# Which branch body stands last, and when the last head groups' transposes are issued: an attention and gated-unit backward kernel on one core

## The chip, the cores and the metric

The kernel runs on one core of a Trainium2 chip. The metric is device time in microseconds (us), the median of several executions. The kernel before takes 4947.9 us. "The profile" is one traced execution of a kernel, some 2 us shorter than the measured time, since it counts from the first to the last instruction.

## The reference, cut to what matters

The program computes a layer and its gradients for 2048 rows of width 576: attention with 32 heads against a given K and V, times a gated unit.

```python
x = A_x
xn = _layernorm(x, axis=-1)
s = _A_ref(xn, A_k_cache, A_v_cache, A_wq, A_wo)   # softmax(q k) v, then wo; 32 heads of 128
g = _silu(_B_ref(xn, B_w_gate, B_w_up, B_w_down))
return x + s * g
...
_out, _vjp = jax.vjp(_f, A_x, A_k_cache, A_v_cache, A_wq, A_wo, B_w_gate, B_w_up, B_w_down)
return (_out0, *_grads)
```

The kernel has four stages: the gated unit forward; attention forward and backward, head by head; the gated unit backward; and last the gradients of `wq` and `wo` and of `x`, in eight groups of four heads.

Of the kernel before, what the change touches and what calls it, by code (L numbers as in the profile page):

```python
# [17 lines left out]
def ldiv(n, m):  # L18
    for d in range(min(n, m), 0, -1):
        if n % d == 0:  # L20
            return d
    return 1
# [44 lines left out]
def kernel(  # L67
# [6 lines left out]
    nc = tc.nc  # L74
# [159 lines left out]
    with tc.tile_pool(name="pa", bufs=1) as pa:  # L234
# [271 lines left out]
        with tc.tile_pool(name="a2h", bufs=3) as hp, \  # L506
# [4 lines left out]
            for sg in range(NT // SG):  # L511
# [7 lines left out]
                for sl in range(SG):  # L519
                    st = sg * SG + sl  # L520
# [343 lines left out]
                slot += 1  # L864

    flag = nc.values_load(flag_i[0:1, 0:1], min_val=0, max_val=1, skip_runtime_bounds_check_because="a comparison gives 0 or 1")
    with tc.If(flag > 0) as branch:
        attention(True)
    with branch.Else():
        attention(False)  # L870
    pdT.release()

    def late(name, bufs=1, **kw):
        return tc.tile_pool(name=name, bufs=bufs, reuse_waits="tile", **kw)
# [4 lines left out]
    HG = ldiv(H, 4)  # L879
    NHG = H // HG  # L880
    WD = ncs[-1][0] + 512
    with late("pc") as pc, late("pcf") as pcf, \
# [127 lines left out]
        def padded(pool, n, nm):  # L1010
            ts_ = [pool.tile([P, DT * P], bf, name=f"{nm}{k}") for k in range(n)]
            if KPAD:
                for t_ in ts_:
                    nc.gpsimd.memset(t_[:, D:], 0.0)
            return ts_

        def carve(t_, pat, a, b):
            v = t_.rearrange(pat)
            assert a * b <= v.shape[1]
            return v[:, :a * b].rearrange("p (a b) -> p a b", b=b)  # L1020

        HC = HG * P
        ds_all = carve(doBT[:], "p a b -> p (a b)", NT, D)
        onb0 = carve(doB[:], "p a b -> p (a b)", NT, HC)
        wqT = carve(wdT2[:], "p a b c -> p (a b c)", HG, D)

        def load_on(on_, hg):
            nc.gpsimd.dma_start(on_, rows_view(on2_d, hg * HC, HC))

        def load_dq(dq_, hg):  # L1030
            nc.gpsimd.dma_start(dq_, rows_view(dq2_d, hg * HC, HC))
# [16 lines left out]
        def turn_rows(dst, src, a, b, n):  # L1048
            nc.sync.dma_start_transpose(dst[:, a * n:b * n, :], src[:, a:b, :].rearrange("p t f -> p (t f)"))  # L1049
# [111 lines left out]
        with late("c2w") as wp, late("c2b") as blk, late("c2s", 2) as sb, late("c2ps", 4, space=PSUM) as ps:  # L1161
            dqTs = padded(wp, 2, "dqT")
            onqs = [(onb0, dqb_at.get(0)), tuple(blk.tile([P, NT, HC], bf, name=nm)[:] for nm in ("onb", "dqb"))]
            if not dqb_at:
                onqs[0] = (onb0, carve(ah0[:], "p a t f -> p (a t f)", NT, HC))
                load_dq(onqs[0][1], 0)
            NTE = NT // 2 if NHG > 1 else 0
            if NHG > 1:
                load_on(onqs[1][0], 1)
                load_dq(onqs[1][1], 1)  # L1170
            dqbT = blk.tile([P, NT * HG, P], bf, name="dqbT")
            dqbT2 = blk.tile([P, max(1, NTE) * HG, P], bf, name="dqbT2")
            wqT2 = blk.tile([P, HG, D], bf, name="wqT2")

            def dx_more(st, both=False):
                acc = ps.tile([P, WD], f32, name="acc")
                terms = [(dqbT[:, st * HG + hl, :], wqT[:, hl, :]) for hl in range(HG)]
                if both:
                    terms += [(dqbT2[:, st * HG + hl, :], wqT2[:, hl, :]) for hl in range(HG)]
                dx_row(acc, st, terms)  # L1180
                return acc

            gots = {}

            def load_got(st):
                gots[st] = sb.tile([P, D], bf, name="got")
                nc.gpsimd.dma_start(gots[st][:], go2[st * P:(st + 1) * P, :])

            def finish(st, acc):
                tot = sb.tile([P, D], f32, name="tot")  # L1190
                cs = sb.tile([P, 2], f32, name="cs")
                junk = sb.tile([P, D], f32, name="junk", bufs=1)
                nc.vector.scalar_tensor_tensor(tot[:], acc[:, :D], 1.0, dxn[:, st, :], op0=ALU.mult, op1=ALU.add, accum_out=cs[:, 0:1])  # L1193
                nc.vector.scalar_tensor_tensor(junk[:], tot[:], 1.0, xn_all[:, st, :], op0=ALU.mult, op1=ALU.mult, accum_out=cs[:, 1:2])  # L1194
                m12 = sb.tile([P, 2], f32, name="m12")
                nc.vector.tensor_scalar(m12[:], cs[:], -1.0 / D, None, op0=ALU.mult)
                nb_ = sb.tile([P, 1], f32, name="nb")
                nc.vector.tensor_tensor(nb_[:], m12[:, 0:1], rstd_all[:, st:st + 1], op=ALU.mult)
                t = sb.tile([P, D], f32, name="t")
                nc.vector.scalar_tensor_tensor(t[:], xn_all[:, st, :], m12[:, 1:2], tot[:], op0=ALU.mult, op1=ALU.add)  # L1200
                nc.scalar.activation(t[:], t[:], AF.Identity, bias=nb_[:], scale=rstd_all[:, st:st + 1])  # L1201
                dx = sb.tile([P, D], bf, name="dx")
                nc.vector.tensor_tensor(dx[:], t[:], gots.pop(st)[:], op=ALU.add)  # L1203
                nc.gpsimd.dma_start(o1[st * P:(st + 1) * P, :], dx[:])

            NQ = max(1, NT // 4)
            for hg in range(NHG):
                cols = slice(hg * HC, (hg + 1) * HC)
                onb, dqb = onqs[hg % 2]
                final = hg == NHG - 1  # L1210
                early = hg == NHG - 2
                ends = list(range(NTE)) if early else list(range(NTE, NT)) if final else []
                nc.sync.dma_start_transpose(wqT, A_wq[:, cols])  # L1213
                def turn_dq(a, b):
                    for a_ in range(a, b, NQ):
                        turn_rows(dqbT, dqb, a_, min(a_ + NQ, b), HG)
                turn_dq(NTE if final else 0, NTE if early else NT)
                if early:
                    nc.sync.dma_start_transpose(wqT2[:], A_wq[:, (hg + 1) * HC:(hg + 2) * HC])
                    turn_rows(dqbT2, onqs[(hg + 1) % 2][1], 0, NTE, HG)  # L1220
                dwq = wp.tile([P, DT, HC], bf, name="dwq")
                for st in ends[:2]:
                    load_got(st)
                nsteps, step_n = 2 * HG, 0
                wait_n = min(3 if early else 1, nsteps - 2)
                todo_rows = list(ends)
                held = []

                def ends_rows():
                    if todo_rows and step_n >= wait_n:  # L1230
                        for _ in range(-(-len(todo_rows) // max(1, nsteps - step_n - final))):
                            if todo_rows:
                                st = todo_rows.pop(0)
                                finish(st, dx_more(st, early))
                                if st + 2 <= ends[-1]:
                                    load_got(st + 2)
                for hl in range(HG):
                    h = hg * HG + hl
                    lcols = slice(hl * P, (hl + 1) * P)
                    accumulate(ps.tile([P, WD], f32, name="acc"), dqb, xn_all, lcols, dqTs[h % 2])  # L1240
                    nc.sync.dma_start_transpose(dwq[:, :, lcols], dqTs[h % 2][:])
                    if early and hl == min(1, HG - 1):
                        turn_dq(NTE, NT)
                    if final and hl == HG - 1:
                        store_T(out_4, cols, dwq)
                    step_n += 1
                    ends_rows()
                    dwo = sb.tile([P, D], bf, name="dwo")
                    accumulate(ps.tile([P, WD], f32, name="acc"), onb, ds_all, lcols, dwo)
                    nc.gpsimd.dma_start(out_5[h * P:(h + 1) * P, :], dwo[:])  # L1250
                    step_n += 1
                    if hl < HG - 1:
                        ends_rows()
                if not final:
                    if hg + 2 < NHG:
                        load_on(onb, hg + 2)
                        load_dq(dqb, hg + 2)
                    store_T(out_4, cols, dwq)
                    for st in range(len(ends), NT):
                        acc = dx_more(st)  # L1260
                        nc.vector.tensor_tensor(dxn[:, st, :], acc[:, :D], dxn[:, st, :], op=ALU.add)
                while todo_rows:
                    step_n = nsteps
                    ends_rows()
# [30 lines left out]
```

## The kernel before: what the change touches

Attention exists twice in the program. The usual body uses no maximum in the softmax, which is safe if a bound on the scores is small. A flag computed on the chip says so. On these inputs the usual body always runs.

```python
flag = nc.values_load(flag_i[0:1, 0:1], min_val=0, max_val=1, ...)
with tc.If(flag > 0) as branch:
    attention(True)       # the usual body
with branch.Else():
    attention(False)      # the general body
```

Right after it the next stage starts: rows of `o` are transposed by DMA, and the rows of `wo` of the last nine heads (in the tiles Kn, Vn, dOn) are loaded, behind a tiny pacing copy that holds the third `o` row back.

```python
for st in range(1, R0):
    if st > 1:
        nc.gpsimd.tensor_copy(oTs[st][0:1, 0, 0:1], loads[0][st % 3][0:1, 0:1])
    load_oT(oTs[st], st)
for view, h0, n, dead in wo_parts:
    if dead in (1, 2, 3):
        load_wo_rows(view, h0, 0, n)
```

The last stage, for each group `hg` of four heads. `wqT` holds transposed weights and `dqbT` transposed rows of dq; both come by transposing DMAs that SyncE issues, one after another.

```python
nc.sync.dma_start_transpose(wqT, A_wq[:, cols])
...
turn_dq(NTE if final else 0, NTE if early else NT)
if early:                     # the last but one group also does half the rows of the last
    nc.sync.dma_start_transpose(wqT2[:], A_wq[:, (hg + 1) * HC:(hg + 2) * HC])
    turn_rows(dqbT2, onqs[(hg + 1) % 2][1], 0, NTE, HG)
...                           # 8 accumulations of 3.9 us, with rows of dx between them
if hg + 2 < NHG:
    load_on(onb, hg + 2)      # 2 MB each
    load_dq(dqb, hg + 2)
```

## Time and profile before

| | before |
|---|---|
| median of 4 runs | 4947.94 us (4942.96 to 4948.41) |
| span of the profiled run | 4943.5 us |
| TensorE busy | 4877.6 us |
| fetch gap at the end of attention | 4.3 us on TensorE, 7.0 us on GpSimd |
| waits for transposed dq in the last two groups | 3.8 and 2.4 us |

The lines themselves stand in the prediction below. How to read them: TensorE (PE in the profile) is busy for 4877.6 of 4943.5 us, so a change is worth what it takes from the time in which TensorE stands still or runs at half clock (the granted clock is 0.50 from 3544 to 3546 us, after the gap at the end of attention, and 1.00 from 3530 to 3542 us). Time on any other engine counts only if TensorE waits for it. In the lines, PEld is TensorE's loading of weights, ACT is ScalarE, DVE VectorE, POOL GpSimd, and SPq the queue of SyncE.

### The profile page before, as it was taken

The numbers are of one execution on the slowest core, as the hardware profiler recorded it, in microseconds if no ns is written. First come the engines' busy times: TensorE is split into PE (matmuls) and PEld (weight loads), VectorE is DVE, ScalarE is ACT, GpSimd is POOL, SyncE is SP. The second block draws the span as 40 slices with busy tenths as digits, with TensorE's granted clock in tenths as the row PEclk, the third lists the DMA queues.
The fourth block names the chain that finished last, engine by engine and source line by source line (L and its number), as shares of the span: only waits on it lengthen the run. The fifth ranks groups of instructions, "written<-read, shape, count | busy, mean of one in ns | idle before, by whom it ended". The sixth has DMA issues, their size and how long they took to land. (4 is left out here: it accounts for less than half of the span.)

```text
span 4943.5 us, 101621 instructions
## 1 busy us (share of the span) xinstructions
PE 4877.6 (99%) x41029; PEld 2892.8 (59%) x41029; DVE 2802.9 (57%) x6554; ACT 2473.9 (50%) x4228; POOL 843.4 (17%) x1329
## 2 busy tenths in 40 slices
PE   9999999999999999999999999999899999999998
PEld 4445666666666666666666666666455555555554
DVE  4544666666566666666656666666434555554225
ACT  4431766766676676676666667667312111111011
POOL 3322111111111111111111111111221111111111
PEclk9999999999999999999999999999999999999999
DMA  7887999999999999999999999999999999998665
GB/s 260 274 202 173 225 222 225 228 229 230 222 231 224 230 225 237 219 227 220 235 220 231 233 224 229 231 221 231 210 225 235 223 234 218 233 226 204 195 168 151
DMA packets 3048181, 1097.68 MB, mean 222 GB/s; under 512 B 2951890, under 2 KB 2956115, under 8 KB 3047699
## 3 DMA queue, kind: packets, MB, share of 16 engines
q1 hardware_dynamic: 2948930, 771.66, 83.4%
q0 software_dynamic: 98160, 318.85, 20.3%
q8 instruction: 322, 5.28, 0.4%
q14 instruction: 161, 1.31, 0.1%
q10 hardware_dynamic: 608, 0.59, 0.0%
HBM read 175.31 MB, written 177.93 MB: 71 GB/s over the span
## 5 line engine op out<-in xcount | busy, mean ns | idle before, releaser
L654 ACT ACTIVATE Pq<-sp 128x1024 bf16<-128x1024 f32 x1024 | 1048.0, 1024 | 268.7 <-PE sp L636 259.4
L709 DVE SCALAR_TENSOR_TENSOR Pq<-dp,negdelta,Pq 128x1024 bf16<-128x1024 f32 x512 | 655.2, 1280 | 44.5 <-PE dp L706 44.5
L712 ACT ACTIVATE t<-dp,negdelta 128x1024 bf16<-128x1024 f32 x512 | 567.6, 1115 | 214.3 <-PE dp L706 199.8
L636 PE MATMUL sp<-KQ 128*128 128x512 bf16 x2048 | 609.6, 379 | 2.2 <-ACT Pq L654 2.1
L706 PE MATMUL dp<-VT,dOT 128*128 128x512 bf16 x2048 | 609.2, 379 | 2.3
L683 PEld LDWEIGHTS <-dST 128*128 128x128 bf16 x8192 | 506.8, 98 | 155.5 <-DMA dST<-Pq 16.3
L683 PEld LDWEIGHTS <-PT 128*128 128x128 bf16 x8192 | 499.8, 98 | 133.6 <-DMA PT<-Pq 14.1
L683 PE MATMUL acc<-Kn,dST 128*128 128x128 bf16 x8192 | 556.3, 219 | 9.0 <-DMA dST<-Pq 8.8
L683 PE MATMUL acc<-Vn,PT 128*128 128x128 bf16 x8192 | 542.0, 219 | 8.6 <-DMA PT<-Pq 8.3
L713 DVE TENSOR_TENSOR Pq<-t,Pq 128x1024 bf16<-128x1024 bf16 x512 | 354.6, 693 | 319.3 <-ACT t L712 307.0
L744 PE MATMUL acc<-Pq,dOn 128*128 128x512 bf16 x2048 | 531.1, 379 | 0.0
L744 PE MATMUL acc<-Pq,Qn 128*128 128x512 bf16 x2048 | 526.7, 380 | 0.0
L724 ACT ACTIVATE dq_n<-acc,rsc 128x128 bf16<-128x128 f32 x512 | 187.7, 367 | 335.1 <-PE acc L683 313.6
L1154 DVE TENSOR_TENSOR dxn<-acc,dxn 128x576 f32<-128x576 f32 x272 | 206.1, 758 | 248.1 <-PE acc L1054 248.1
L744 PEld LDWEIGHTS <-Qn 128*128 128x128 bf16 x2048 | 200.4, 98 | 240.8 <-issue 1.5
L744 PEld LDWEIGHTS <-dOn 128*128 128x128 bf16 x2048 | 198.9, 98 | 233.8
L1116 ACT ACTIVATE ndh<-dh 128x512 bf16<-128x512 f32 x144 | 86.0, 597 | 452.5 <-DVE du_blk L1114 448.7
L641 DVE TENSOR_REDUCE rs_all<-rsp 128x1 f32<-128x2 f32 x512 | 78.4, 153 | 306.4 <-ACT Pq L654 294.8
L636 PEld LDWEIGHTS <-KQ 128*128 128x128 bf16 x2048 | 179.3, 98 | 124.4 <-issue 4.0
L706 PEld LDWEIGHTS <-dOT 128*128 128x128 bf16 x2048 | 178.7, 98 | 124.6 <-issue 12.4
L677 POOL DMA_DIRECT2D on_d<-o_n x128 | 97.4, 761 | 784.3 <-DVE junk L695 460.3
L677 POOL DMA_DIRECT2D dq_d<-dq_n x128 | 98.2, 768 | 721.4 <-ACT dq_n L724 681.7
(208 smaller groups left out, 6827.6 us busy)
## 6 DMA issues: line engine op xcount, KB each, us to landing
out_dram<-kvn POOLq DMA_DIRECT2D x64, 512.0 KB, 4.8
ah<-a_d POOLq DMA_DIRECT2D x18, 1024.0 KB, 9.3
ah<-h_d POOLq DMA_DIRECT2D x18, 1024.0 KB, 11.7
h_d<-h_row POOLq DMA_DIRECT2D x64, 256.0 KB, 3.5
a_d<-a_row POOLq DMA_DIRECT2D x64, 256.0 KB, 3.9
x_all<-in_A_k_cache_dram SPq DMA_DIRECT2D x64, 256.0 KB, 4.0
on_d<-o_n POOLq DMA_DIRECT2D x128, 128.0 KB, 4.6
kvT_d<-KQ POOLq DMA_DIRECT2D x32, 512.0 KB, 5.7
```

Of the source, the lines that this page charges most:

```text
L636: nc.tensor.matmul(sp[:, c * CH:(c + 1) * CH], lhsT=hs.QT[:, qt * P:(qt + 1) * P], rhs=hs.KT[:, hf * HW_ + c * CH: hf * HW_ + (c + 1) * CH ...
L654: nc.scalar.activation(Pq[:, hsl], sp[:], AF.Exp, scale=SCALE, accum_out=hs.rsp[:, hf:hf + 1])
L677: nc.gpsimd.dma_start(dst_d[q0 * P:(qt + 1) * P, hs.h * P:(hs.h + 1) * P].rearrange("(t p) d -> p t d", p=P), buf[:])
L683: nc.tensor.matmul(hs.acc[:, 0, :], lhsT=T[:, kt, :], rhs=rhs[:, kt, :], start=(kt == 0), stop=(kt == NT - 1))
L706: nc.tensor.matmul(dp[:, c * CH:(c + 1) * CH], lhsT=hs.dOT[:, qt * P:(qt + 1) * P], rhs=hs.VT[:, hf * HW_ + c * CH: hf * HW_ + (c + 1) * C ...
L709: nc.vector.scalar_tensor_tensor(Pq[:, hsl], dp[:], hs.negdelta[:, qt:qt + 1], Pq[:, hsl], op0=ALU.add, op1=ALU.mult)
L712: nc.scalar.activation(t[:], dp[:], AF.Identity, bias=hs.negdelta[:, qt:qt + 1], scale=1.0)
L713: nc.vector.tensor_tensor(Pq[:, hsl], t[:], Pq[:, hsl], op=ALU.mult)
L724: nc.scalar.activation(hs.dq_n[:, qt % G4, :], hs.acc[:, 0, :], AF.Copy, scale=hs.rsc[:, qt:qt + 1])
L744: nc.tensor.matmul(self.acc, lhsT=self.nat[:, qt, :], rhs=self.slabs[qt][:, cs], start=(qt == self.lo), stop=(qt == self.hi - 1))
L1116: nc.scalar.mul(ndh[:], dh[:], -1.0)
L1154: nc.vector.tensor_tensor(dxn[:, st, :], acc[:, :D], dxn[:, st, :], op=ALU.add)
```

## The change

It has two parts with one intent: to remove the last places where TensorE waits for something that could have come sooner. The first lets the usual body stand last, so that its end runs straight into the next stage, where there was a jump over the general body. The second issues the transposes for the last group a group sooner, and uses their weights again instead of loading them a second time.

```diff
-    with tc.If(flag > 0) as branch:
+    with tc.If(flag < 1) as branch:
+        attention(False)
+    with branch.Else():
         attention(True)
-    with branch.Else():
-        attention(False)
...
+            def last_turns():
+                nc.sync.dma_start_transpose(wqT2[:], A_wq[:, (NHG - 1) * HC:])
+                turn_rows(dqbT2, onqs[(NHG - 1) % 2][1], 0, NTE, HG)
...
-                nc.sync.dma_start_transpose(wqT, A_wq[:, cols])
+                if not (final and NTE):
+                    nc.sync.dma_start_transpose(wqT, A_wq[:, cols])
...
-                if early:
-                    nc.sync.dma_start_transpose(wqT2[:], A_wq[:, (hg + 1) * HC:(hg + 2) * HC])
-                    turn_rows(dqbT2, onqs[(hg + 1) % 2][1], 0, NTE, HG)
...
-                                finish(st, dx_more(st, early))
+                                finish(st, dx_more(st, early, wqT2[:] if final and NTE else wqT))
...
+                if hg == NHG - 3:
+                    last_turns()
```

More of the change, by code (lines that the diff above doesn't have):

```diff
@@ L1173, with dx_more @@
             wqT2 = blk.tile([P, HG, D], bf, name="wqT2")
-            def dx_more(st, both=False):
+            def last_turns():
+                nc.sync.dma_start_transpose(wqT2[:], A_wq[:, (NHG - 1) * HC:])
+                turn_rows(dqbT2, onqs[(NHG - 1) % 2][1], 0, NTE, HG)
+            def dx_more(st, both=False, w=wqT):
                 acc = ps.tile([P, WD], f32, name="acc")
-                terms = [(dqbT[:, st * HG + hl, :], wqT[:, hl, :]) for hl in range(HG)]
+                terms = [(dqbT[:, st * HG + hl, :], w[:, hl, :]) for hl in range(HG)]
                 if both:
@@ L1206 @@
             NQ = max(1, NT // 4)
+            if NHG == 2:
+                last_turns()
             for hg in range(NHG):
@@ L1261 @@
                         nc.vector.tensor_tensor(dxn[:, st, :], acc[:, :D], dxn[:, st, :], op=ALU.add)
+                if hg == NHG - 3:
+                    last_turns()
                 while todo_rows:
```

## The prediction

> **What bounds the kernel now.** I read the page first. It says that TensorE decides nearly everything: 99% of the span is matmul, so only what makes TensorE stand still, or run at a lower clock, can be won. Span minus PE busy is 4943.5 - 4877.6 = 65.9 us for the whole program.
>
> ```profile
> span 4943.5 us, 101621 instructions
> PE 4877.6 (99%) x41029; PEld 2892.8 (59%) x41029; DVE 2802.9 (57%) x6554; ACT 2473.9 (50%) x4228; POOL 843.4 (17%) x1329
> ```
>
> The waits view of PE (columns: who waits, for whom, us in total, times, longest) then says where it stands still. Two of its lines belong to the two parts of the change; two more hang on the first.
>
> ```profile
> PE acc L1054 <- DMA dqbT<-dqb: 6.2, 2, 3.8
> PE acc L958 <- issue: 5.4, 2, 4.3
> PE acc L958 <- DMA Vn<-in_A_wo_dram: 3.8, 1, 3.8
> PE acc L958 <- DMA Kn<-in_A_wo_dram: 1.8, 1, 1.8
> ```
>
> Then the timeline around the end of attention (start us, us long, engine, line, operation, in brackets the idle time before it and what ended it). "issue" means that no semaphore explains the idle time. TensorE does 20 matmuls, stands for 4.31 us, then runs slowly; GpSimd stands for 6.98 us.
>
> ```profile
> 3536.07 2.61 PE L958 MATMUL acc<-dsT,KQ 128*128 128x512 bf16 x20 [1.07 <-issue]
> ...
> 3542.99 2.81 PE L958 MATMUL acc<-dsT,KQ 128*128 128x512 bf16 x14 [4.31 <-issue]
> ...
> 3543.62 0.56 POOL L933 DMA_DIRECT2D dsg<-dsg_d  x1 [6.98 <-issue]
> ...
> 3560.08 1.60 PE L958 MATMUL acc<-Vn,KQ 128*128 128x512 bf16 x6 [3.77 <-DMA Vn<-in_A_wo_dram]
> ```
>
> The packets of the instruction queues (page part 3 lists them, q8 in 16 KB packets, q14 in 8 KB ones) settle what this is: one 16 KB packet at 3539.6 us lasting 2.0 us, and three 8 KB packets at 3539.4 to 3539.6. The engines had run out of instructions. They jump from the end of the first branch body over the second, which for PE is 53,720 instructions long.
>
> The entry into attention, by contrast, falls through, and nothing of the kind is seen: PE goes straight on, and its first wait is for ScalarE.
>
> ```profile
> 483.24 0.59 PE L636 MATMUL sp<-KQ 128*128 128x512 bf16 x2
> ...
> 485.07 1.28 ACT L612 ACT_TABLE_LOAD   x1 [1.29 <-PE acc L215]
> ...
> 487.63 0.59 PE L636 MATMUL sp<-KQ 128*128 128x512 bf16 x2 [2.12 <-ACT Pq L654]
> ```
>
> Last, the timeline of the two last head groups, where SyncE issues transposing DMAs one behind the other.
>
> ```profile
> 4830.01 3.62 SPq L1213 DMA_TRANSPOSE wdT<-in_A_wq_dram  x1
> ...
> 4833.73 3.80 SPq L1049 DMA_TRANSPOSE dqbT<-ah  x2
> ...
> 4837.58 2.33 SPq L1219 DMA_TRANSPOSE wqT<-in_A_wq_dram  x1
> ...
> 4840.01 4.33 SPq L1049 DMA_TRANSPOSE dqbT<-dqb  x1
> ...
> 4846.52 1.16 PE L1054 MATMUL acc<-wqT,dqbT 128*128 128x512 bf16 x8 [3.80 <-DMA dqbT<-dqb]
> ...
> 4890.54 2.14 SPq L1213 DMA_TRANSPOSE wdT<-in_A_wq_dram  x1
> ...
> 4896.82 2.13 PE L1054 MATMUL acc<-wdT,dqbT 128*128 128x512 bf16 x16 [2.39 <-DMA dqbT<-dqb]
> ```
>
> [...] after 3.80 us of waiting the next 24 matmuls take 4.79 us in the chain of waits, where 24 take 24 x 15.68/128 = 2.94 us at full clock; after the 2.39 us wait they keep full speed. [...]
>
> **The change part by part.** No arithmetic is added or removed. The order of instructions, laid side by side, is the same on every engine inside both attention bodies; after them SyncE has one DMA fewer (367 instead of 368) and four rows in another order.
>
> *A. Exit from attention.* The usual body now stands last. A branch instruction still ends it, but its target is the next instruction. Removed from PE: 1.07 + 4.31 = 5.4 us standing, and the slow stretch after it: 26 matmuls from 3542.99 to 3547.8 took 4.85 us, at half clock, so some 2.4 us more. What counts, though, is what comes next: PE then waits for Kn, Vn and dOn rows, which GpSimd loads after a pacing copy at 3547.43. So the gain is what GpSimd gains. It finishes its last store at 3536.64 and could go on at once instead of at 3543.62: up to 6.9 us. Its row loads would now queue behind a 512 KB store in flight (it landed 7.6 us after issue) and the transposes of xnT, so I take off 1 us: the copy comes at about 3541.4, and Kn, Vn and dOn land as long after it as now (7.5 to 12 us). The waits for Kn and Vn, 5.6 us, stay. Gain 6 us, between 4 and 7.
>
> *B. Entry.* The jump moves here, and all five engines take it. Each fetch costs (from the exit: packet landed at 3541.6, PE on at 3543.0) about 1.4 us after landing, plus 0.3 to 2 us of packet[...]. Around 482 us only GpSimd's stores are moving, and no transposes, so I estimate 2.5 to 3 us for an engine, not 7. PE would start at about 485 instead of 482.9, but its next wait is for ScalarE anyway (2.12 us). ScalarE ends its last work at 483.79 and loads its table only at 485.07, since it also waits for stores issued at 482.2; so about 1.3 us of its fetch is hidden. Net delay 1.4 us through ScalarE[...]. [...] Cost 2.5 us, between 0.5 and 5.
>
> *C. Last head groups.* Today, between 4830.0 (the group before has done with its weights) and PE's need of the first row at 4842.7, SyncE must issue 3.62 + 3.80 + 2.33 + 4.33 = 14.1 us of transposes. After: the weights of the last group go out at about 4812, when SyncE is idle. The turn of its dq rows needs a load issued at 4817.0 that lands 14.3 us later by the tile view of dqb:
>
> ```profile
> L1031 POOL DMA_DIRECT2D dqb<-dq_d x1: 1163/1163/1163, 4817.0 to 4817.0; - x1
> ...
> DMA to landing us min/median/max: 14.3/14.3/14.3
> ```
>
> So it starts at 4831.3, no sooner than PE frees the weights, and holds SyncE for 4.3 us (to 4835.7). Weights of the group, 2.5 to 3.6 us, follow to 4838.2 to 4839.4; the first turn is issued then and lands 4.0 us later (as the one at 4892.77 did): 4842.2 to 4843.4, against a need at 4842.7. The wait shrinks from 3.80 to 0 to 0.7 us, and with it the 1.85 us of half clock (4.79 - 2.94). Gain 5.65 less 0.4, say 5.2, between 3 and 5.7.
>
> In the last group the reload of weights (2.14 us) is gone, because the weights lie in a second tile. The first turn need no longer wait for the last row of the previous group, so it can go out some 4 us earlier. The 2.39 us wait vanishes: gain 2.4. VectorE then still has eight rows of 4.36 us = 34.9 us, which today run from 4898.0 to 4932.9 without a break, so the end follows VectorE's first row, and that moves with PE's. The tail after it (ScalarE's last casts, the dwq transpose, stores) is unchanged. C together: 7.6 us.
>
> **Sum.** -6 + 2.5 - 7.6 = -11.1 us; 4947.64 - 11.1 = 4936.5. The rivals are mostly on the small side, so I say 4937.
>
> **The rivals.**
> 1. *The jump is only moved.* The fetch at the entry costs as much as at the exit (PE 5.4 us and 2.4 us of low clock). For it: all engines fetch at once[...]. Against it: little DMA traffic and a ScalarE wait that hides some. A and B then cancel, leaving C: 4940.
> 2. *The branch that ends the second body still refetches*, although its target is adjacent. [...] A is then nothing and B is paid: 4947.64 + 2.5 - 7.6 = 4942.5.
> 3. *Head-of-line blocking on SyncE.* The early turn waits for its 2 MB load, and the weights stand behind it in the same queue. If that load lands at 4835 rather than 4831.3, the first turn lands at about 4846.5 as today, and only the 2.4 us of the last group remain: 4942.
> 4. *A second hidden wait at the exit:* rows queue behind the 512 KB store, and A gains only 3 us: 4940.
>
> **Range and chances.** Taking the low ends (A 7, B 0.5, C 8.1) gives 4933; A 4, B 5, C 5.4 gives 4943. The three times of the kernel before differ by 5.3 us among themselves, so I widen to 4930 to 4945. All this is 0.2% of the span; neither rival comes near 2% (99 us). Faster by over 2%: 0.01; within 2%: 0.98; slower: 0.01.
>
> **What would show it.** A right: no "issue" gap on the first L958 matmuls, GpSimd's first row load about 0.1 us after its last store, waits for Kn and Vn still there. B right: instruction packets at about 482 to 486 us, an "issue" gap of 2 to 3 us on PE, table load at about 486.5. C right: the L1054 wait for dqbT under 1 us in total, matmuls after it at full speed, one weight transpose fewer. I am wrong if the gap at the entry exceeds 5 us, if the exit keeps its gap, or if the early turn holds up the weights beyond 4840.

B's 2.5 us of cost were 1.4 us through ScalarE and about 1 us for a lower TensorE clock; this second term was the author's estimate. The sum: -6 + 2.5 - 7.6 = -11.1 us.

## The result, and the profile after

The changed kernel takes 4934.34 us (4931.75 to 4937.6, 4 runs) against 4947.94 us. The ratio is 0.9975, with a 95% interval of 0.9958 to 0.9992. A ratio here is the mean time of one kernel's runs over that of the other's runs of the same rounds, so it is not quite the ratio of the medians. The gain of some 12 to 14 us is real but small.

The page of the profile after, its first lines:

```profile
span 4929.9 us, 100847 instructions
...
PE 4835.4 (98%) x40273; PEld 2894.6 (59%) x41029; DVE 2802.5 (57%) x6554; ACT 2472.1 (50%) x4228; POOL 840.7 (17%) x1329
```

Careful here: PE busy fell by 42 us, more than the span. But 756 matmul records are missing (40273 of 41029), so this row shows nothing of the change. Weight loads (PEld) are complete in both, so I compare the traces by the start of the same weight load in each.

The waits view of PE after (who waits, for whom, total us, times, longest):

```profile
PE sp L636 <- issue: 5.2, 2, 2.7
PE acc L958 <- DMA Kn<-in_A_wo_dram: 2.8, 1, 2.8
PE acc L958 <- DMA Vn<-in_A_wo_dram: 2.8, 1, 2.8
PE acc L1054 <- DMA dqbT<-ah: 1.6, 1, 1.6
...
PE acc L958 <- issue: 0.2, 1, 0.2
```

The "issue" wait has moved from L958 (the exit from attention) to L636 (the entry). The dqbT waits, 6.2 us in two before, are one of 1.6 us.

The timeline at the entry, after:

```profile
485.50 0.39 PE L636 MATMUL sp<-KQ 128*128 128x512 bf16 x1 [2.50 <-issue]
486.52 1.28 ACT L612 ACT_TABLE_LOAD   x1 [2.86 <-DMA dsg_d<-dsg]
...
488.56 0.61 PE L636 MATMUL sp<-KQ 128*128 128x512 bf16 x1 [2.67 <-issue]
...
489.20 1.02 ACT L654 ACTIVATE Pq<-sp 128x1024 bf16<-128x1024 f32 x1 [1.18 <-PE sp L636]
```

TensorE stops twice: after the branch, and again after one matmul. 16 KB instruction packets begin at 482.5 and 486.2 us, within these two gaps. ScalarE's first exponential starts at 489.2, where before it started at 486.5.

The timeline at the exit, after:

```profile
3533.59 4.33 PE L958 MATMUL acc<-dsT,KQ 128*128 128x512 bf16 x33
...
3534.85 0.55 POOL L756 DMA_DIRECT2D kvT_d<-VT  x1 [1.81 <-DVE VT L754]
...
3535.39 0.55 POOL L933 DMA_DIRECT2D dsg<-dsg_d  x1
...
3552.16 1.60 PE L958 MATMUL acc<-Vn,KQ 128*128 128x512 bf16 x6 [2.76 <-DMA Vn<-in_A_wo_dram]
```

TensorE runs on at full speed (33 matmuls in 4.33 us, granted clock 1.00 from 3533 to 3540 us), and GpSimd issues its next load the moment its last store is out. The waits for the `wo` rows in Kn and Vn are still there.

The exit before, shown in the prediction, had two fetches as well. TensorE's branch is on record there at 3532.25 us for 3.65 us, with a 16 KB packet at 3533.2; after it TensorE stood only 1.07 us. The gap of 4.31 us came 41 instructions later (20 matmuls, 21 weight loads), with the next packet at 3539.6. In turns_only and reload_only (below) it comes after the same 41 instructions. So this stop seems tied to its place in the program, as the second stop at the entry is, which padding removes (pad, below). No run here moves the one at the exit, so its cause is not shown.

The timeline of the last but one group, after:

```profile
4824.37 4.64 SPq L1049 DMA_TRANSPOSE dqbT<-dqb  x1
...
4829.11 2.29 SPq L1220 DMA_TRANSPOSE wdT<-in_A_wq_dram  x1
...
4831.45 4.96 SPq L1049 DMA_TRANSPOSE dqbT<-ah  x2
...
4836.22 1.15 PE L1054 MATMUL acc<-wdT,dqbT 128*128 128x512 bf16 x8 [1.62 <-DMA dqbT<-ah]
```

(The tile names are those of reused memory: wdT is the weight tile, ah the dq rows.) SyncE now has three jobs in this stretch instead of four, and has issued the last by 4836.4. The matmuls after the short wait run at full speed, 8 in 1.15 us.

From the aligned weight loads, in us. "Entry" is from the last weight load before the branch to the 120th after it; "attention" from there to its last weight load; "exit" from there to the first of the gated unit's backward stage; then that stage and the first six groups; the last two groups; and the end.

```
                 entry attention    exit  middle   group6  group7     end     span
before            22.3    3029.3   147.4  1148.0     60.5    41.5    11.7   4943.5
after             24.0    3026.5   141.5  1148.0     56.7    39.0    11.6   4929.9
```

So: entry +1.7, exit -5.9, the last two groups -3.8 and -2.5, together -10.5 us. The rest of the 13.6 us comes from attention itself (-2.8), in which the two kernels do the same; the repeated run below shows that this part is chance.

### The profile page after: what moved, and what is told of

The parts are those of the page before. It is cut to its first block, busy times and chain, and to the rows that moved or that the text cites. A ratio compares the mean times of both kernels' runs of the same rounds, so it can differ in the third digit from the quotient of the medians.

```text
span 4929.9 us, 100847 instructions
## 1 busy us (share of the span) xinstructions
PE 4835.4 (98%) x40273; PEld 2894.6 (59%) x41029; DVE 2802.5 (57%) x6554; ACT 2472.1 (50%) x4228; POOL 840.7 (17%) x1329
## 4 chain that ended last, share of the span: by engine, by line
PE 94%; DMA 2%; DVE 2%; issue 1%; ACT 1%; SPq 0%; POOL 0%; POOLq 0%; ACTq 0%; DVEq 0%
PE acc L683 18%; PE acc L744 18%; PE acc L998 13%; PE acc L1054 8%; PE dp L706 8%; PE sp L636 8%; PE acc L215 6%; PE u_ps L450 3%; PE dh L1111 3%; PE g_ps L448 3%; PE acc L533 3%; PE acc L958 2%; PE acct L145 1%; DMA dST<-Pq 1%; DVE Pq L709 1%
## 5 line engine op out<-in xcount | busy, mean ns | idle before, releaser
L706 PE MATMUL dp<-VT,dOT 128*128 128x512 bf16 x1919 | 581.6, 379 | 2.4
L683 PEld LDWEIGHTS <-PT 128*128 128x128 bf16 x8192 | 500.1, 98 | 130.9 <-DMA PT<-Pq 11.1
L636 PE MATMUL sp<-KQ 128*128 128x512 bf16 x1858 | 568.9, 380 | 5.2 <-issue 5.2
L636 PEld LDWEIGHTS <-KQ 128*128 128x128 bf16 x2048 | 179.3, 98 | 127.7 <-issue 7.2
```

The source lines that it names most:

```text
L636: nc.tensor.matmul(sp[:, c * CH:(c + 1) * CH], lhsT=hs.QT[:, qt * P:(qt + 1) * P], rhs=hs.KT[:, hf * HW_ + c * CH: hf * HW_ + (c + 1) * CH ...
L683: nc.tensor.matmul(hs.acc[:, 0, :], lhsT=T[:, kt, :], rhs=rhs[:, kt, :], start=(kt == 0), stop=(kt == NT - 1))
L706: nc.tensor.matmul(dp[:, c * CH:(c + 1) * CH], lhsT=hs.dOT[:, qt * P:(qt + 1) * P], rhs=hs.VT[:, hf * HW_ + c * CH: hf * HW_ + (c + 1) * C ...
```

## The experiments

Theory: the jump costs a fetch wherever it is taken, and it is cheaper at the entry than at the exit; the two parts of the change act each on its own stretch and add. Rivals: the jump is only moved and gains nothing; the branch instruction itself costs, wherever its target; SyncE's queue, not the transfers, sets the time of the turns.

The table collects every trace, in the columns explained above. The middle is left out: it is 1148.0 us everywhere but in all_three, where it is 1148.6. The last column is the last part of attention, 1200 weight loads in the last head.

```
                 entry attention    exit   group6  group7     span  last head
before            22.3    3029.3   147.4     60.5    41.5   4943.5      142.8
after             24.0    3026.5   141.5     56.7    39.0   4929.9      141.4
after_again       24.4    3031.9   140.5     56.1    39.0   4934.2      145.0
branch_only       24.2    3040.4   141.2     62.0    43.4   4952.5      147.3
turns_only        21.2    3030.5   148.0     56.8    39.0   4937.6      144.7
reload_only       21.3    3038.7   148.3     61.6    39.0   4951.2      147.2
no_else           21.3    3023.4   146.7     56.8    39.0   4929.4      142.6
pad               26.1    3023.3   141.0     58.8    39.0   4931.0      144.6
dq_first          24.5    3027.0   139.7     56.7    39.0   4929.6      142.9
defer_on          24.3    3024.6   138.9     54.9    39.0   4924.0      139.9
late_rows         24.6    3034.6   134.8     56.8    39.2   4932.1      145.1
all_three         24.1    3028.4   129.8     56.6    39.3   4921.7      144.6
rows_defer        24.3    3037.1   129.8     54.9    39.0   4927.7      150.8
pad_rows_defer    24.8    3032.9   129.8     54.9    39.0   4923.4      149.0
```

### The two parts, each alone: branch_only and turns_only

branch_only is the kernel before with this edit and nothing else:

```diff
-    with tc.If(flag > 0) as branch:
-        attention(True)
-    with branch.Else():
-        attention(False)
+    with tc.If(flag < 1) as branch:
+        attention(False)
+    with branch.Else():
+        attention(True)
```

> Only the order of the two attention bodies is swapped; the last head groups stay as in the kernel before. My theory (entry costs about 1.7 us in the aligned traces, exit gains about 7.2 us): net 5 to 6 us faster than before apart from the attention part itself, whose own waits moved by up to 4 us either way between the two first traces; no 'issue' gap of over 0.3 us on the first L958 matmuls, two 'issue' gaps on L636 of 2.5 to 2.7 us each, and the two dqbT waits of 3.8 and 2.4 us still there. Rival 'the jump is only moved': net 0 to 1 us.

turns_only is the changed kernel with that edit undone.

> Only the turns of the last head groups are changed; the usual body stays first and jumps at its end. My theory: the two dqbT waits (3.8 and 2.4 us) become one of about 1.6 us, no half clock after it, and the last two groups end 6 to 7 us sooner; the exit keeps its 'issue' gap of some 4 us on L958 and 7 us on GpSimd. Net 6 to 7 us faster than before. Rival: the gain hangs on the shifted phase of the exit, then under 4 us.

Measured: branch_only 4940.19 us, ratio to before 0.9988 (0.9972 to 1.0005); turns_only 4939.25 us, ratio 0.9987 (0.9971 to 1.0004). Each is a gain of some 6 us, and each interval just reaches 1, so the times alone don't settle it. The traces do. In branch_only the entry is 24.2 and the exit 141.2, as in the changed kernel, while the last groups are as before or worse. In turns_only it is the other way round. Its waits of PE:

```profile
PE acc L958 <- issue: 5.3, 2, 4.2
...
PE acc L1054 <- DMA dqbT<-ah: 1.7, 1, 1.7
```

The fetch gap at the exit is back, and the dqbT wait is the short one. The two ratios fall short of 1 by 0.0012 and 0.0013, together 0.0025, which is what the whole change has. With intervals of 0.0017 to either side, so exact a sum is luck; that each part changes its own stretches, and only it does, is what the traces show.

The profiled run of branch_only was its slowest (4954.25; the other three 4936.66 to 4943.13). It shows where the scatter is: its attention took 3040.4 us, 11 more than before.

### Half of the second part: reload_only

The kernel before, in which the last group uses the second weight tile and doesn't load its weights again; the early turns stay where they were.

```diff
-                nc.sync.dma_start_transpose(wqT, A_wq[:, cols])
+                if not (final and NTE):
+                    nc.sync.dma_start_transpose(wqT, A_wq[:, cols])
...
-                                finish(st, dx_more(st, early))
+                                finish(st, dx_more(st, early, wqT2[:] if final and NTE else wqT))
```

> Of the head group part only this: the last group uses the second weight tile and does not load its weights again; the early turns stay where they were. My theory: the 2.4 us wait in the last group goes to 0 (1.9 us or more gained there), the 3.8 us wait and the half clock after it stay. Rival: the wait in the last group is one for the dq turn itself, issued when the last row is done; then 2 us of it stay.

Measured: one look, 4952.96 us, with an attention of 3038.7. The last group takes 39.0 us, just as in the whole change, and the wait in it is gone; the one in the group before it stays:

```profile
PE acc L1054 <- DMA dqbT<-dqb: 4.1, 1, 4.1
```

So the last group's 2.5 us come from not loading the weights again, and the 3.8 us of the group before come from issuing the turns sooner.

### Is it the branch or the distance: no_else

The changed kernel without the general body. It is no usable kernel, but on these inputs its result is right. The compare-and-branch and the closing branch are still there.

```diff
-    with tc.If(flag < 1) as branch:
-        attention(False)
-    with branch.Else():
-        attention(True)
+    with tc.If(flag > 0):
+        attention(True)
```

> The changed kernel with the general body left out altogether: compare-and-branch and the closing branch remain, but neither goes far (the result stays right on these inputs; it is no usable kernel). If the cost at the entry is the fetch of a distant target: no 'issue' gap on L636, ScalarE's first exponential at about 486.4 us instead of 489.2, and everything up to the first head 1.7 us sooner than in the changed kernel; exit as in the changed kernel. Rival (the branch instruction itself flushes what was fetched): a gap of 2.5 us or more stays at the entry.

Measured: 4931.65 us, ratio 0.9975. At the entry:

```profile
484.77 1.28 ACT L612 ACT_TABLE_LOAD   x1 [1.27 <-DMA dsg_d<-dsg]
...
487.32 0.59 PE L636 MATMUL sp<-KQ 128*128 128x512 bf16 x2 [2.10 <-ACT Pq L654]
```

No "issue" gap is left, and the entry takes 21.3 us, as in the two kernels with the usual body first (21.2 and 21.3; 22.3 in the first trace of before). Which branches there are the traces tell too (`--source L867`; on TensorE, in before, after and no_else; ns shortest, median and longest, then first and last start):

```profile
L867 PEldq COMPARE_BRANCH  x2: 92/1870/3647, 481.5 to 3532.3; - x2
...
L867 PEldq COMPARE_BRANCH  x1: 4018/4018/4018, 481.4 to 481.4; - x1
...
L867 PEldq COMPARE_BRANCH  x2: 87/136/185, 481.2 to 3525.1; - x2
```

The two records of 3.65 and 4.02 us are the jumps over a whole body. At the entry of before and no_else the branch falls through (92 and 87 ns). The closing branch of no_else goes nowhere far (185 ns on TensorE, 38 to 51 on the others), and no fetch gap follows. The changed kernel has no branch at the exit at all. So it is the jump over the body that costs, not the branch instruction. The fetch at the entry costs 24.3 - 21.5 = 2.8 us (the mean of the seven unpadded kernels that jump there, and of the four that don't).

A miss: the exit should have been 141 us and was 146.7, with no fetch gap. The waits for Kn and Vn were 4.9 and 8.9 us there; the Vn rows landed 18.8 us after their issue, against 10.7 in the changed kernel. Why, no run here tells. This cost 5 us, more than the 2.8 us that leaving out the jump gained; that no_else still ran as fast as the changed kernel goes with its attention of 3023.4 us.

### The second stop at the entry: pad

TensorE stopped again after one matmul, with a 16 KB packet before each of its two stops (482.5 and 486.2 us). If the second stop hangs on where the target of the jump lies among these packets, moving the target would remove it. That was a guess. The edit adds 16 instructions to the general body, which never runs:

```diff
+            if not fast:
+                pad = acc_tile(bf)
+                for _ in range(8):
+                    nc.tensor.transpose(pad[:, 0, :], ident[:], ident[:])
```

> The changed kernel with 16 more TensorE instructions (8 transposes that never run) at the end of the general body. In the changed kernel PE stopped twice at the entry, after 0 and after 2 instructions, with an instruction packet before each[...]. Theory: with the target moved 16 on, [...] one 'issue' gap of about 2.5 us stays and the second one (2.7 us) goes; the first 120 weight loads after the entry take about 22.8 us instead of 24.0, since ScalarE (table load near 486.5) then binds. Rival: ScalarE's and GpSimd's fetches bind anyway, then no change in the 24.0 us.

Measured: one look, 4932.76 us. The second stop is gone, as the two PE lines with a wait at the entry show:

```profile
485.49 0.59 PE L636 MATMUL sp<-KQ 128*128 128x512 bf16 x2 [2.41 <-issue]
...
489.19 0.59 PE L636 MATMUL sp<-KQ 128*128 128x512 bf16 x2 [1.60 <-ACT Pq L654]
```

So it went, here and in the two later kernels with padding: each has one gap, where the seven unpadded kernels with a jump at the entry have two. So where the target lies matters here; why it does is not shown. The gain did not come: the entry took 26.1 us, not 22.8. ScalarE's table load began at 486.6, as without padding (486.5). Its own fetch is the likely cause: the profile puts the 2.86 us in the changed kernel down to a store, but behind the same store, without a jump, no_else loaded at 484.77. ScalarE's first exponential came 1.2 us sooner (488.0 against 489.2), but TensorE then waited 3.4 us for the first transposes of P, which it had not done in the changed kernel. In the two later kernels with padding the entry took 24.1 and 24.8. So the rival stands: removing a stop that wasn't the last to end gained nothing here.

### What bounds the early turns: dq_first and defer_on

In the changed kernel SyncE stood until 4824.4 for a 2 MB load of dq rows, while TensorE had been done with the old weights at about 4822.8. That looked like head-of-line blocking. dq_first puts that load first:

```diff
-                        load_on(onb, hg + 2)
                         load_dq(dqb, hg + 2)
+                        load_on(onb, hg + 2)
```

> The changed kernel with the two loads for the group after next in the other order, dq rows before o rows. Theory (head-of-line blocking: SyncE stood until 4824.4 for the dq load issued second, while PE had freed the weights at 4822.8): the dq load lands some 5 us sooner, the remaining 1.6 us wait for dqbT goes to 0 to 0.3 us, and the stretch of the last but one group falls from 56.7 to 55.1 us. Rival: the o rows, now second, land too late for the group's second accumulation, and a new wait of 1 to 3 us appears on L998; or the transposes themselves are too slow and 1 us or more stays.

Measured: one look, 4931.43 us. The load landed after 9.0 us instead of 14.5, and SyncE started the early turn at once:

```profile
4817.39 11.38 SPq L1049 DMA_TRANSPOSE dqbT<-dqb  x1
...
4828.87 2.17 SPq L1220 DMA_TRANSPOSE wdT<-in_A_wq_dram  x1
```

The turn now took 11.38 us instead of 4.64 and ended at the same time as before (the weights follow at 4828.9; in the changed kernel, 4829.1). The wait stayed at 1.7 us. My theory fell: the order of the two loads is not the bound. The new theory is that the 2 MB load of o rows beside the turn takes the bandwidth: the turn got 6.7 us longer when that load was issued second. defer_on tests it by moving that load of the last group behind the turns:

```diff
+                        if hg != NHG - 3:
+                            load_on(onb, hg + 2)
-                        load_on(onb, hg + 2)
...
                     if early and hl == min(1, HG - 1):
                         turn_dq(NTE, NT)
+                        load_on(onqs[(NHG - 1) % 2][0], NHG - 1)
```

> The changed kernel with the load of the last group's o rows (2 MB) put off until after the turns of the group before last. Loading dq first did not help: the load landed 5 us sooner, but the early turn then took 11.4 us instead of 4.6 and ended at the same time. Theory: what bounds the turns is the DMA engines' throughput between about 4808 and 4829 us, shared with the 4 MB of loads. Then with 2 MB taken out of that stretch the dqbT wait (1.6 us) goes to 0 to 0.3 and the stretch of the last but one group falls from 56.7 to 55.1 us, if the o rows still land before the last group needs them. Rival: SyncE's own issue time of the transposes bounds; then 1 us or more of the wait stays.

Measured: one look, 4925.77 us.

```profile
4815.23 4.23 SPq L1049 DMA_TRANSPOSE dqbT<-dqb  x1
...
4830.40 1.15 PE L1054 MATMUL acc<-wdT,dqbT 128*128 128x512 bf16 x8
```

The turn is about as short as it was in before (4.23 us, against 4.33), TensorE has no wait before its first row, and the group takes 54.9 us instead of 56.7. The o rows landed 10.2 us after their later issue, and the last group is unchanged at 39.0. So the DMA engines' throughput bounds the turns here, as expected: 11.38 us with the o load moved behind the dq load, 4.23 with it out of the stretch. In dq_first the DMA engines were full from 4812 to 4828 us (mean busy share of 1.01 to 1.25 in each 4 us, as the profile counts it). There one transfer was sooner at the other's cost: the dq load took 5.5 us less to land than in the changed kernel (9.0 against 14.5), the turn 6.7 us more (11.38 against 4.64).

### The waits behind the exit: late_rows, and the edits together: all_three

The exit still had 5.5 us of waiting for `wo` rows in Kn and Vn and 1.2 us for the third `o` row, and half clock after them (6 matmuls in 1.60 us; at full clock 0.90). late_rows loads these rows within the last head, where the other 23 heads' rows are loaded already, and drops the pacing copy.

```diff
-                if dead in (1, 2, 3):
-                    continue
                 view_h0[id(view)] = h0
...
-                if st > 1:
-                    nc.gpsimd.tensor_copy(oTs[st][0:1, 0, 0:1], loads[0][st % 3][0:1, 0:1])
                 load_oT(oTs[st], st)
-            for view, h0, n, dead in wo_parts:
-                if dead in (1, 2, 3):
-                    load_wo_rows(view, h0, 0, n)
```

> The changed kernel with the last nine heads' rows of wo loaded inside the last head's attention, as the other 23 are, and without the pacing copy before the third transposed row of o. Theory: the waits for Kn, Vn and xn_all after the exit (2.8, 2.8, 1.2 us) and the half clock that follows them go, and the stretch from the last attention matmul to the first of the next stage falls from 141.5 us to about 131; net 9 to 11 us faster than the changed kernel, some 20 us than before. Rival: the loads delay the transposes of the last head (more dST waits there), or the third o row becomes the wait instead (over 4 us on xn_all); then under 4 us.

all_three is the changed kernel with pad, dq_first and late_rows together.

> The changed kernel with the three edits together (16 instructions of padding, dq loads first, wo rows inside attention). If each acts alone on its own stretch, the gains add: about 1 + 1.6 + 10 us, so some 12 us under the changed kernel and 24 us (0.5%) under the one before. If one is absorbed by another, under 8 us.

Measured: late_rows 4937.03 us (4929.36 to 4940.49), ratio to before 0.9971; all_three 4926.7 us (4920.73 to 4927.64), ratio 0.9949 (0.9936 to 0.9963). The three waits are gone in both, and the exit falls from 141.5 to 134.8 and 129.8 us. In late_rows one new wait appears some 28 us into the exit:

```profile
3569.74 5.64 PE L951 MATMUL acc<-dsT,KQ 128*128 128x512 bf16 x31 [3.26 <-DMA KQ<-on_d]
```

The o row after those came late there; in the three other kernels with this edit it didn't. The net gain of late_rows over the changed kernel, expected at 9 to 11 us, can't be seen in its times: its attention took 3034.6 us, 8 more than in the first trace of the changed kernel. all_three shows the expected 24 us against before (0.9949 of 4951 is 25 us less), but two of its three edits did nothing by themselves, so chance in attention is part of it.

### What repeats, and a version that may beat both: after_again, rows_defer, pad_rows_defer

after_again is the changed kernel, unedited.

> The changed kernel once more, unedited, for a narrower interval and to see what repeats. Theory: about 0.25% faster than the kernel before; entry (first 120 weight loads) 24 us, exit to the next stage 141 us, last two groups 56.7 and 39.0 us, as in its first trace, while the attention in between differs by several us from the first trace. Rival: these stretches vary as much as the attention does, and the split of the gain was luck.

rows_defer is the changed kernel with late_rows and defer_on.

> The changed kernel with both edits that are left: the wo rows loaded inside attention (exit stretch 134.8 and 129.8 us instead of 141.5 in the two runs that had it) and the o rows' load put off. Theory: 8 to 13 us under the changed kernel of the same call, some 20 to 25 us (0.4 to 0.5%) under the one before. Rival: the extra loads lengthen the waits for dST in the last head and give back what the exit gained; then under 5 us.

Measured, 5 rounds: after_again 4936.02 us, ratio 0.9974 (0.9961 to 0.9988); rows_defer 4929.64 us, ratio 0.9966 (0.9952 to 0.9979). Before ran between 4940.14 and 4955.13 in the same rounds. after_again repeats the first result, and its stretches too: 24.4, 140.5, 56.1, 39.0. Its attention took 3031.9 us, 2.6 more than before, where the first trace had 2.8 less. So attention scatters by itself. The traces' attention runs from 3023.3 to 3040.4 us; the scatter of the times (15 us for before) is of that size.

rows_defer has both stretches as expected (129.8 and 54.9), but its last head took 150.8 us, and the 6 us between the two medians fall short of the expected 8 to 13. Is that chance, or do the extra loads lengthen it? pad_rows_defer, with the padding added, asks again.

> The version with wo rows inside attention and the late load of o rows, plus the 16 instructions of padding. Theory: padding gives nothing (in both runs that had it, ScalarE's fetch and table load set the entry), so this is the version without it again: ratio to the kernel before 0.995 to 0.997, exit stretch 118.1 + 11.7 us, last but one group 54.9 us, and the last head's stretch, 150.8 us without padding, back within the 140 to 147 us of the other runs if that value was chance. Rival: the loads of wo rows do lengthen the last head; then it is above 148 us again.

Measured: 4926.02 us (4925.34 to 4935.43), ratio 0.9965 (0.995 to 0.9981). Its last head took 149.0 us, so by what I had written down the rival holds. The four kernels that load the rows inside the last head took 145.1, 144.6, 150.8 and 149.0 us there, mean 147.4; the ten others 139.9 to 147.3, mean 143.8. Some 3.5 us of the 12 us that the exit gained are given back in the last head. With so few traces and such scatter this is likely, not certain.

So rows_defer, with or without padding, is faster than before. Against the changed kernel it is better by its stretches and its median, by some 6 us against after_again in the same rounds, but the two intervals overlap: that it is faster is likely, not shown.

## Why the prediction was right

**Size.** 4937 us was said, with 4930 to 4945; 4934.34 was measured. "Within 2%" was right.

**A, exit.** Said: 6 us gained, the waits for Kn and Vn unchanged at 5.6 us. The exit stretch lost 5.9 us, and the two waits sum to 5.5. The way there was right too: the pacing copy came 4.8 us after GpSimd's last store (3540.22 against 3535.40), as the prediction had it. What the copy and the row loads take after the store, and not TensorE's own gap with its half clock, set the gain. Two readings were wrong without harm. The half clock had cost some 1.7 us, not 2.4: 26 matmuls took 4.85 us, and at the full clock, in the changed kernel, 46 take 5.6, so 26 take 3.2. And no branch ends the second body; the changed kernel's trace has none there.

**B, entry.** Said: cost 2.5 us, TensorE on at 485, table load at 486.5. Measured: 485.5 and 486.52; the cost is 1.7 us against the first trace of before and 2.8 us between the means of the kernels with and without a distant jump there. GpSimd stood 4.00 us, more than the 2.5 to 3 estimated for an engine; whether less DMA traffic makes it shorter than the 6.98 us at the exit is not shown. The granted clock was lower: 0.58 on average from 486 to 494 us, against 0.79 in before. A second stop, named as a possibility in a passage now cut, did come after two instructions (2.67 us, with a 16 KB packet at 486.2 us), and pad shows that removing it gained nothing. One reading doesn't hold: in before the profile puts ScalarE's wait of 1.29 us down to TensorE, not to the stores, of which the last had landed 2.6 us after its issue, at 484.8. Rival 1 fails by its size. Rival 2 can't be judged from the changed kernel, which has no closing branch, but no_else has one, with a near target and no fetch gap. Rival 4 fails too: Kn landed 7.1 us after its issue, where it took 7.5 before.

**C, last groups.** The last group's 2.4 us came as 2.5. The last but one gained 3.8 us where 5.2 was said, still within the stated 3 to 5.7. Here two terms were mis-sized. The need was put at 4842.7, when TensorE began to wait before. But before, it had already done the first 8 matmuls of that row and waited for the second half; now what lands last is needed by the first 8, so the need is 1.0 us sooner. And the first turn landed 4.8 us after issue (4831.45 to 4836.2), not 4.0. The two make 1.8 us; the wait was 1.62. The start and duration of the early turn were as said (14.5 us to land, 4.64 us to turn). The half clock went with the wait: the granted clock was 0.74 on average from 4846.5 to 4853 us in before, after 3.80 us of waiting, and is 1.00 from 4830 to 4846.5 us in the changed kernel, around the 1.62 us. Rival 3, blocking in the queue, looked likely from this trace, but dq_first and defer_on (turns of 11.38 and 4.23 us) show that bandwidth is behind it.

**The sum.** -11.1 us was said. The four stretches give -10.5. That this is so near is partly luck: C fell 1.3 us short, and B cost 0.8 us less in this trace. The difference to the measured 13.6 is attention, with 2.8 us in this trace and the other sign in after_again. The repeated measurement, ratio 0.9974, is 12.9 us of 4948. What the prediction did not see is how large this scatter is: it had only 5.3 us between three runs of before, and later calls showed 15 and more.

## What to carry to other kernels

The jump over the long body made TensorE and GpSimd stand at whichever end it was taken: TensorE for 5.4 us at the exit of before and 5.2 us at the entry of the changed kernel, GpSimd for 6.98 and 4.00 us. ScalarE likely stood too, at the entry (2.86 us before its table load, against 1.27 in no_else). Put the jump where some engine would wait anyway (here TensorE waited 2.12 us for ScalarE at the entry of before), and count the gain on the engine whose work is needed next, not on the one with the widest gap. When moving DMAs earlier, look at what else moves in that stretch: here reordering two large transfers only traded one for the other (a load 5.5 us faster, a turn 6.7 us slower), and moving one out of the stretch helped (54.9 us for the group instead of 56.7). When a gain is 0.2%, compare the traces stretch by stretch at the same instruction, because the scatter of the whole run hides it.
